# The first MLP's scale and offset, applied where its sums are copied out of PSUM

## The chip, the cores and the metric

One core of one Trainium2 chip runs the whole program. The metric is the device time of one execution in microseconds. Three runs of the kernel before took 1071.02, 1076.27 and 1076.54 us, so the median is 1076.27 us.

## The reference

Attention over 4 sequences of 576 positions with 8 heads of 64, then two MLPs over 2304 tokens of 512 features. What matters here is the first MLP.

```python
def _moe_ref(x, w_in, w_out, s, b):
    h = x @ w_in                 # 2304x512 @ 512x2048
    r = np.maximum(h, 0.0)
    g = s * (r * r) + b          # s and b are one number each
    return (g @ w_out).astype(np.float32)   # 2048x512

def _moe2_ref(x, w_a, w_b, w_out):
    return ((x @ w_a) * (x @ w_b) @ w_out).astype(np.float32)
```

Since s and b are single numbers, `g @ w_out` equals s times `(r * r) @ w_out` plus b times the sum of each column of `w_out`.

## The kernel before, in words

Tokens are cut into six units of 384 (`TB`, `NB` = 6), and the 2048 inner features of the first MLP into 16 steps of 128 (`NF1`). For each unit and step, `h_mm` (lines 538 to 557) multiplies x by a step of `w_in`. Every float32 operand of the large products is split into a high and a low part (`split`, lines 104 to 106: the high part is copied on ScalarE, the low one is a subtraction on the engine that is named), and a product is three products of TensorE, so a step's h is 12 products of 128x128 by 128x384. Behind them stands a chain over the value `r`: ScalarE takes the positive part (line 550) and squares it (line 551), GpSimd applies s and b (line 552), ScalarE copies the high part into `gt`, and VectorE subtracts the low part (lines 105 and 106). This chain has a raised priority. `o_mm` (lines 559 to 573) then multiplies `gt` by the step of `w_out`, 12 products again, and adds them up in four PSUM banks over all 16 steps; it follows h by two steps (`AHEAD1`). After the last step ScalarE copies the four banks out (line 572), and SyncE's queue stores them to memory, feature by token; the last unit keeps a tile of its own.

The weights arrive as float64. `stage` (lines 108 to 121) loads a step as pairs of words, `to_float32` (lines 123 to 148) turns them to float32 in place in the high words, with a scaling on ScalarE (for the second MLP on GpSimd, line 128), three bit operations on VectorE (lines 137, 140, 143), and a split whose low part is GpSimd's. `next_weights` (lines 693 to 698) does this for both matrices, for two steps before unit 0 and for one step in each step of unit 0. The staged words lie in slots that the finished weights use later; the last steps have two slots of another pool (`raw`).

Alongside the first MLP runs the attention of the next unit, which VectorE and GpSimd share: GpSimd multiplies (lines 477 and 495), VectorE sums (lines 481 and 506), and the results become the next unit's x. `Stream` deals its steps out evenly over the calls in a unit. In the last unit the attention is over, and the weights of the second MLP are loaded and turned to float32 (`load_w2`), with low parts and scaling on GpSimd. The second MLP follows: 12 inner steps for each of the six units, 36 products in a step.

Each engine works through its queue in an order that is fixed when the program is built: a planner simulates the program and takes the ready instruction of the highest priority. Instructions of different engines are tied by semaphores alone.

Of the kernel before, what the change touches and what calls it, by code (L numbers as in the profile page):

```python
# [8 lines left out]
F32 = mybir.dt.float32  # L9
F32R = mybir.dt.float32r  # L10
U32 = mybir.dt.uint32
AF = mybir.ActivationFunctionType
ALU = mybir.AluOpType
# [4 lines left out]
P = 128  # L18
# [3 lines left out]
# takes the exponent that the high word of 2.0 ** -119 has, read as a float32, to the least one  # L22
# [4 lines left out]
def sparse_attention_two_mlps(  # L27
# [14 lines left out]
    """Rows of x are tokens.  Heads 0-3 see the last 32 positions, heads 4-7 the  # L42
    earlier positions of their own residue modulo 32.

    Every float32 operand of the large products is split into hi (12 significant
    bits, float32r) and lo = value - hi (exact), and a product is hi*hi + hi*lo +
    lo*hi, accumulated in float32.  The weights come as the bits of float64 and
    are made float32 by shifting their fields into place.
    """
    nc = tc.nc  # L50
    B, H, S, D = q.shape
    NT, DM = out.shape
# [5 lines left out]
    QT = 96  # L58
# [29 lines left out]
    # window column c is allowed for row p where p < c <= p + 32  # L88
# [12 lines left out]

    o1 = dram.tile([DM, NT], F32, name="o1")
# [5 lines left out]
    def stage(w, f, cols, pool):  # L108
        """A part of a matrix of float64 as (low, high) words; also the load's instruction."""
# [13 lines left out]
    def to_float32(r, pool, tag, on_pool=False):  # L123
        """(low, high) words of float64 -> hi and lo parts of the float32."""
        low, high = r[:, :, 0], r[:, :, 1]
        # what is below float32's range gets a zero exponent here, the others keep their low bits
# [9 lines left out]
        # the sign stays; the exponent's three upper bits, now zero, go  # L136
# [16 lines left out]
    # post-processing goes before what else is ready  # L153
# [3 lines left out]
    # ------------------------------------------------------------- attention  # L157
# [6 lines left out]
    # the part that no head of the stride sees is set once  # L164
# [5 lines left out]
    # each head's query rows, zero in the other's  # L170
# [3 lines left out]
    def softmax(pt, scores, msk):  # L174
        """pt = exp(scale * (scores + msk) - max) / (sum + 1e-9) along the last axis."""
# [50 lines left out]
    def local(spans, n, hp_, c0):  # L226
        """A pair of heads for two spans (sequence, first position) of queries; two neighbours
        in a partition.  Keys of spans that follow each other are shared."""
# [73 lines left out]
    def first_mask():  # L302
        """For the first positions of a sequence: heads 0-3's, then heads 4-7's."""
# [21 lines left out]
    def first(bb, qk, vn, fmask, pool, tag):  # L325
        """All heads of a sequence's first positions."""
# [49 lines left out]
    def strided_one(pair):  # L376
        """Two strided heads of all sequences' second QT positions: sequence and residue in the
        partitions, two heads for each step."""
# [47 lines left out]
        # [(b r), (h d)] -> [(h d), (b r)] for each step  # L426
# [9 lines left out]
    def strided_soft(pt, sc, rows, cols):  # L436
        """pt = softmax of scale * sc along the last axis."""
# [17 lines left out]
    def pairs(u):  # L455
        # (first column, columns, first row): two columns at a time where all rows see them
        i0 = (u % NP) * IU
        for j in range(0, i0, 2):
            yield j, 2, 0
        for j in range(IU):  # L460
            yield i0 + j, 1, j

    def strided(u):
# [23 lines left out]
        def strided_rest():  # L487
# [23 lines left out]
            # [(h r), (i, d)] -> [(i parity, d), (h r)], two steps i at a time  # L511
# [23 lines left out]
    # ------------------------------------------------------------- first MLP  # L535
    wi, wo = {}, {}

    def h_mm(n, f):
# [9 lines left out]
        with tc.high_priority(offset=URGENT):  # L548
# [3 lines left out]
            nc.gpsimd.tensor_scalar(  # L552
                out=r, in0=r, scalar1=s_sb, scalar2=b_sb, op0=ALU.mult, op1=ALU.add
            )
# [4 lines left out]
    def o_mm(acc, gt, f, n):  # L559
# [10 lines left out]
        for e in range(KD):  # L570
            o = hp.tile([P, TB], F32, tag="r", name="o1s", bufs=3) if last is None else last[:, e]
            nc.scalar.activation(out=o, in_=acc[e], func=AF.Copy)
            nc.sync.dma_start(out=o1[e * P:(e + 1) * P, cols], in_=o)

    # ------------------------------------------------------------- second MLP
# [3 lines left out]
    def load_w2(i):  # L579
        f, kind = divmod(i, 3)  # L580
        # the slots that stage the others' words take the last ones
# [225 lines left out]
```

## Time and profile before

| | |
|---|---|
| runs | 1071.02, 1076.27, 1076.54 us |
| profiled execution, from its first to its last instruction | 1073.5 us |
| TensorE busy | 984.4 us, 92% |
| VectorE busy | 610.7 us, 57% |
| ScalarE busy | 415.4 us, 39% |
| GpSimd busy | 494.2 us, 46% |
| mean granted clock of TensorE | 0.961 of 2.4 GHz |

The profile's own record of the profiled execution is its span; the median of the runs lies 2.8 us above it. An engine's busy time includes time in which an instruction has begun and waits for something inside the engine. TensorE's two rows are the products (PE) and the loading of weights into its array (PEld), which overlap. A wait is the idle time of an engine ahead of an instruction, with the instruction that ended it.

### The profile page before, as it was taken

The page shows a single profiled execution, that of the slowest core. Times are in us where ns is not written, and L with a number is a line of the kernel's source. Part 1 is how long each engine was busy: PE and PEld are TensorE (multiplying, and loading weights), DVE is VectorE, ACT ScalarE, POOL GpSimd, SP SyncE. Part 2 cuts the span into 40 slices and gives each one's busy share as a digit, 9 for nine tenths or more (in the row PEclk, how much of TensorE's full clock was granted, in tenths as well). Part 3 has the DMA queues.
Part 4 walks back from the last instruction along what each step waited for, and adds up shares of the span by engine and source line. Part 5 has one row for each costly group of instructions (what it writes and reads, how often), then busy time and mean ns, then how long its engine had stood idle before and what let it go on. Part 6 is the DMA issues. An engine that isn't in the chain of part 4 may idle for free.

```text
span 1073.5 us, 14660 instructions
## 1 busy us (share of the span) xinstructions
PE 984.4 (92%) x5382; PEld 914.5 (85%) x5382; DVE 610.7 (57%) x1128; ACT 415.4 (39%) x1075; POOL 494.2 (46%) x428
## 2 busy tenths in 40 slices
PE   7867789988989999999987789999999999999998
PEld 6767678888979889898876778999999999999997
DVE  6899988898895885884789992111211111111111
ACT  5665655535535545645534341211211211211211
POOL 1599787887784885862789980100100100100000
PEclk9988889989999999999989899999999999999999
DMA  8753731121211121102344550010200100000000
GB/s 158 219 179 100 198 84 60 40 50 35 58 35 32 49 52 31 56 13 85 98 157 147 157 173 5 30 30 1 59 1 2 59 1 1 30 1 1 30 1 30
DMA packets 98888, 68.33 MB, mean 64 GB/s; under 512 B 57856, under 2 KB 92928, under 8 KB 98816
## 3 DMA queue, kind: packets, MB, share of 16 engines
q1 hardware_dynamic: 98816, 67.40, 22.4%
q8 instruction: 42, 0.69, 0.3%
q14 instruction: 30, 0.25, 0.1%
HBM read 57.93 MB, written 9.44 MB: 63 GB/s over the span
## 4 chain that ended last, share of the span: by engine, by line
PE 54%; DVE 18%; POOL 15%; issue 7%; ACT 4%; DMA 2%; SPq 1%; POOLq 0%; DVEq 0%; ACTq 0%
PE acc L621 13%; PE pa L605 13%; PE pb L605 13%; PE acc L562 6%; DVE ot L506 5%; PE h L543 4%; POOL w L106 4%; POOL r L552 4%; POOL prod L477 3%; DVE gt L106 3%; DVE raw L143 2%; POOL raw L128 1%; DVE raw L140 1%; DVE raw L137 1%; POOL prod L495 1%
## 5 line engine op out<-in xcount | busy, mean ns | idle before, releaser
L562 PE MATMUL acc<-gt,w 128*128 128x384 f32 x1152 | 248.6, 360 | 40.8 <-DVE gt L106 22.0
L562 PEld LDWEIGHTS acc<-gt,w 128*128 128x128 f32 x1152 | 214.7, 202 | 55.8 <-DVE gt L106 29.8
L543 PE MATMUL h<-x,w 128*128 128x384 f32 x1152 | 238.1, 351 | 13.1 <-ACT w L105 4.9
L543 PEld LDWEIGHTS h<-x,w 128*128 128x128 f32 x1152 | 207.8, 196 | 19.0 <-ACT w L105 6.9
L613 DVE TENSOR_TENSOR ab<-pb,ab 128x384 f32<-128x384 f32 x72 | 40.1, 556 | 299.8 <-PE pb L605 298.7
L621 PE MATMUL acc<-w,abt 128*128 128x512 f32 x648 | 162.3, 394 | 4.9 <-ACT abt L105 2.5
L605 PE MATMUL pa<-x,w 128*128 128x384 f32 x864 | 164.7, 338 | 0.0
L605 PE MATMUL pb<-x,w 128*128 128x384 f32 x864 | 161.9, 334 | 0.0
L605 PEld LDWEIGHTS pa<-x,w 128*128 128x128 f32 x864 | 154.8, 189 | 6.2
L605 PEld LDWEIGHTS pb<-x,w 128*128 128x128 f32 x864 | 150.8, 188 | 0.3 <-ACT w L105 0.3
L621 PEld LDWEIGHTS acc<-w,abt 128*128 128x128 f32 x648 | 120.2, 188 | 28.5 <-DVE abt L106 3.7
L106 POOL TENSOR_TENSOR x<-xr,x 128x384 fp32r<-128x384 f32 x24 | 26.4, 1126 | 254.5 <-ACT x L105 254.5
L106 POOL TENSOR_TENSOR w<-raw,w 128x512 fp32r<-128x512 f32 x68 | 111.1, 1642 | 29.2 <-ACT w L105 25.1
L552 POOL TENSOR_SCALAR r<-r,s_sb,b_sb 128x384 f32<-128x384 f32 x96 | 102.5, 1068 | 41.4 <-ACT r L551 41.3
L495 POOL TENSOR_TENSOR prod<-sv,pt 128x768 f32<-128x768 f32 (+6 forms) x84 | 92.6, 1109 | 52.5 <-DVE ot L506 26.2
L477 POOL TENSOR_TENSOR prod<-sq,sk 128x768 f32<-128x768 f32 (+6 forms) x84 | 106.7, 1282 | 15.6 <-DVE s L481 11.1
L106 DVE TENSOR_TENSOR gt<-r,gt 128x384 fp32r<-128x384 f32 x96 | 90.4, 944 | 39.7 <-ACT gt L105 39.2
L612 ACT ACTIVATE ab<-pa 128x384 f32<-128x384 f32 x72 | 35.3, 491 | 183.1 <-PE pa L605 183.1
L506 DVE TENSOR_TENSOR ot<-ot,prod 128x384 f32<-128x384 f32 (+2 forms) x104 | 95.4, 917 | 6.3 <-POOL prod L495 0.5
L105 ACT ACTIVATE gt<-r 128x384 fp32r<-128x384 f32 x96 | 50.1, 522 | 107.0 <-POOL r L552 106.7
L105 ACT ACTIVATE abt<-ab 128x384 fp32r<-128x384 f32 x72 | 37.7, 524 | 138.9 <-DVE ab L613 138.9
L105 ACT ACTIVATE w<-raw 128x512 fp32r<-128x512 f32 x68 | 45.5, 675 | 72.2 <-DVE raw L143 60.1
(92 smaller groups left out, 956.4 us busy)
## 6 DMA issues: line engine op xcount, KB each, us to landing
raw<-in_moe_w_out_dram SPq DMA_DIRECT2D x28, 512.0 KB, 4.4
raw<-in_moe_w_in_dram SPq DMA_DIRECT2D x16, 512.0 KB, 5.9
raw<-in_moe_w_a_dram SPq DMA_DIRECT2D x12, 512.0 KB, 3.8
raw<-in_moe_w_b_dram SPq DMA_DIRECT2D x12, 512.0 KB, 3.9
xr<-o SPq DMA_DIRECT2D x6, 768.0 KB, 4.5
o<-o1s SPq DMA_DIRECT2D x20, 192.0 KB, 1.9
vn<-in_v_dram SPq DMA_DIRECT2D x40, 64.0 KB, 2.2
out_dram<-o SPq DMA_DIRECT2D x9, 256.0 KB, 2.1
```

The source lines that it names most:

```text
L105: nc.scalar.activation(out=hi, in_=src, func=AF.Copy)
L106: return eng_lo.tensor_tensor(out=lo, in0=src, in1=hi.bitcast(F32), op=ALU.subtract)
L477: nc.gpsimd.tensor_tensor(out=p_[:, :m, r:], in0=sq[:, None, r:, :].to_broadcast(shape), in1=sk[:, j:j + m, None, :].to_broadcast(shape), ...
L495: nc.gpsimd.tensor_tensor(out=p_[:, :m, r:], in0=sv[:, j:j + m, None, :].to_broadcast(shape), in1=pt[:, r:, j:j + m].rearrange("p i j -> p ...
L506: nc.vector.tensor_tensor(out=ot[:, r:], in0=ot[:, r:], in1=p_[:, e, r:], op=ALU.add)
L543: nc.tensor.matmul(ph, lhsT=wi[f][:, a, kk, :], rhs=x_t[n][:, c, kk, :], start=(m == 0), stop=(m == 3 * KD - 1),)
L552: nc.gpsimd.tensor_scalar(out=r, in0=r, scalar1=s_sb, scalar2=b_sb, op0=ALU.mult, op1=ALU.add)
L562: nc.tensor.matmul(acc[e], lhsT=wo[f][:, a, e * P:(e + 1) * P], rhs=gt[:, c, :], start=(f == 0 and m == 0), stop=(f == NF1 - 1 and m == 2),)
L605: nc.tensor.matmul(pz, lhsT=w2[i][:, a, kk, :], rhs=x2[:, c, kk, :], start=(m == 0), stop=(m == 3 * KD - 1),)
L612: nc.scalar.activation(out=ab, in_=pa, func=AF.Copy)
L613: nc.vector.tensor_tensor(out=ab, in0=pb, in1=ab, op=ALU.mult)
L621: nc.tensor.matmul(acc[t], lhsT=gt[:, a, t * P:(t + 1) * P], rhs=w2[3 * f + 2][:, c, :], start=(f == 0 and m == 0), stop=(f == NF2 - 1 and ...
```

## The change

GpSimd's instruction between the two products is gone, so `gt` holds the square without s and b. While the weights are made, GpSimd adds up the 16 steps of `w_out` in `w_sum` (128x512); after the last one TensorE multiplies it by b, held in all 128 partitions, which gives b times the column sums, and VectorE copies these to `b_col`. The copy out of PSUM multiplies by s and adds `b_col`. Comments are dropped too; they are left out here.

```diff
+    w_sum = const.tile([P, DM], F32, name="w_sum")
+    b_col = const.tile([P, KD], F32, name="b_col")
...
             r = hp.tile([P, TB], F32, tag="r", name="r", bufs=3)
             nc.scalar.activation(out=r, in_=ph, func=AF.Relu)
             nc.scalar.activation(out=r, in_=r, func=AF.Square)
-            nc.gpsimd.tensor_scalar(
-                out=r, in0=r, scalar1=s_sb, scalar2=b_sb, op0=ALU.mult, op1=ALU.add
-            )
             gt = gp.tile([P, 2, TB], F32R, tag="gt", name="gt")
             split(gt[:, 0], gt[:, 1], r, nc.vector)
...
-            nc.scalar.activation(out=o, in_=acc[e], func=AF.Copy)
+            nc.scalar.activation(
+                out=o, in_=acc[e], func=AF.Identity, scale=s_sb, bias=b_col[:, e:e + 1]
+            )
...
         wo[f] = to_float32(words[f][1], wpb, "w")
+        part = words[f][1][:, :, 1].bitcast(F32)
+        if f == 0:
+            nc.gpsimd.tensor_copy(out=w_sum, in_=part)
+        else:
+            nc.gpsimd.tensor_tensor(out=w_sum, in0=w_sum, in1=part, op=ALU.add)
+        if f == NF1 - 1:
+            pc = ps_a.tile([P, KD], F32, tag="a", name="pc")
+            for e in range(KD):
+                nc.tensor.matmul(
+                    pc[:, e:e + 1], lhsT=w_sum[:, e * P:(e + 1) * P], rhs=b_sb, start=True, stop=True,
+                )
+            nc.vector.tensor_copy(out=b_col, in_=pc)
```

## Rows read from the trace of the kernel before

**Rows 1.** The page: busy us (share) xinstructions, and the granted clock in 40 slices.

```profile
PE 984.4 (92%) x5382; PEld 914.5 (85%) x5382; DVE 610.7 (57%) x1128; ACT 415.4 (39%) x1075; POOL 494.2 (46%) x428
...
PEclk9988889989999999999989899999999999999999
```

**Rows 2.** Busy by stretch: from:to, length, PE PEld DVE ACT POOL, clock, DMA.

```profile
39.00:172.00 133.00, 104.28 (x527) 93.25 (x528) 122.73 (x215) 81.54 (x204) 112.91 (x76) 0.86 0.51 145
172.00:260.00 88.00, 78.29 (x460) 74.00 (x459) 76.85 (x139) 40.96 (x121) 68.86 (x63) 0.94 0.18 45
260.00:349.00 89.00, 81.98 (x489) 77.46 (x488) 69.18 (x138) 44.64 (x135) 62.21 (x58) 0.96 0.17 43
349.00:435.00 86.00, 80.38 (x486) 76.78 (x484) 64.87 (x133) 42.66 (x125) 60.83 (x56) 0.96 0.17 43
435.00:519.00 84.00, 80.08 (x487) 75.91 (x485) 58.75 (x127) 45.23 (x134) 47.84 (x49) 0.98 0.16 50
519.00:616.00 97.00, 80.06 (x398) 74.11 (x397) 86.99 (x91) 42.67 (x83) 90.28 (x71) 0.91 0.47 150
616.00:647.00 31.00, 26.09 (x133) 22.86 (x132) 27.69 (x31) 13.12 (x26) 24.17 (x20) 1.00 0.52 162
647.00:1073.50 426.50, 422.05 (x2221) 395.06 (x2219) 76.80 (x136) 84.19 (x169) 17.96 (x17) 1.00 0.05 17
...
60.00:150.00 90.00, 64.99 (x333) 57.25 (x334) 84.51 (x138) 53.96 (x133) 83.74 (x53) 0.84 0.49 136
...
540.00:616.00 76.00, 59.84 (x288) 55.31 (x287) 73.86 (x75) 29.11 (x54) 71.01 (x56) 0.89 0.48 152
```

**Rows 3.** Line 552: ns min/median/max, first and last start; who waited (us, times).

```profile
L552 POOL TENSOR_SCALAR r<-r,s_sb,b_sb x96: 652/960/4993, 46.7 to 608.4; 128x384 f32<-128x384 f32 x96
...
  ACT gt L105: 106.7, 64
```

**Rows 4.** Line 552 alone, by stretch: from:to, length, POOL busy (xcount), clock, DMA.

```profile
39.00:172.00 133.00, 28.15 (x17) 0.86 0.51 145
...
349.00:435.00 86.00, 13.12 (x16) 0.96 0.17 43
...
519.00:616.00 97.00, 22.91 (x16) 0.91 0.47 150
```

**Rows 5.** GpSimd on 128x512: the weights' subtraction, and the scaling of their words.

```profile
L106 POOL TENSOR_TENSOR w<-raw,w x68: 1285/1610/7396, 34.1 to 646.6; 128x512 fp32r<-128x512 f32 x68
...
L128 POOL TENSOR_SCALAR raw<-raw x36: 637/918/1102, 155.4 to 642.3; 128x512 f32<-128x512 f32 x36
```

**Rows 6.** Weight loads' waits, unit 0, then 519 to 647 us: us, times, longest.

```profile
PEld acc L562 <- ACT gt L105: 15.9, 8, 3.5
...
PEld acc L562 <- DVE gt L106: 16.0, 9, 2.9
```

**Rows 7.** The chain that ended last: start us, us, what.

```profile
506.60 2.08 PE h L543 x12
```

**Rows 8.** Weight loads, 172 to 519 us: busy us, mean ns, idle before.

```profile
L562 PEld LDWEIGHTS acc<-gt,w 128*128 128x128 f32 x768 | 139.2, 196 | 13.3 <-DVE gt L106 9.4 <-ACT o1s L572 2.3 <-ACT gt L105 0.9
L543 PEld LDWEIGHTS h<-x,w 128*128 128x128 f32 x750 | 132.5, 193 | 7.1 <-ACT r L550 2.9 <-DVE x L106 2.3 <-ACT x L105 0.8
...
L283 PEld LDWEIGHTS ppt<-ident,lpt 96*128 96x128 f32 x64 | 7.2, 150 | 9.8 <-issue 6.8 <-ACT r L550 2.6
```

**Rows 9.** ScalarE's exponential with a bias, and a plain copy: ns min/median/max.

```profile
L188 ACT ACTIVATE lpt<-lpt,mx x80: 384/388/405, 53.7 to 506.7; 96x128 f32<-96x128 f32 x80
...
L265 ACT ACTIVATE kT<-pqk x80: 260/268/297, 41.5 to 500.1; 64x112 f32<-64x112 f32 x64, 64x128 f32<-64x128 f32 x16
```

**Rows 10.** In order of time near 148 us: SyncE's loads, and GpSimd.

```profile
148.91 2.26 SPq L118 DMA_DIRECT2D raw<-in_moe_w_out_dram  x2
...
147.60 1.29 POOL L106 TENSOR_TENSOR w<-raw,w 128x512 fp32r<-128x512 f32 x1
```

**Rows 11.** VectorE's bit operation on line 140: ns min/median/max.

```profile
L140 DVE SCALAR_TENSOR_TENSOR raw<-raw x68: 643/692/1808, 20.9 to 643.0; 128x512 uint32<-128x512 uint32 x68
```

## The prediction

> **What bounds the kernel now.** Read the totals first [rows 1]: TensorE is busy for 92% of the span, GpSimd for 46%. That alone would say that work on GpSimd is free. It isn't, because the share is a mean over stages with different limits, so the second view cuts the span at the ends of the six units of the first MLP (unit 0 from 39 to 172 us, unit 5 from 519 to 616 us) and shows the second MLP behind them [rows 2]. The reader is to see three kinds of stage.
>
> In unit 0, and above all from 60 to 150 us, VectorE is busy for 84.5 and GpSimd for 83.7 of 90 us, TensorE for 65 [rows 2]: the weights are being turned to float32 there while the attention of the next unit runs, and both engines are full. Unit 5 from 540 to 616 us is the same picture with the weights of the second MLP: 73.9 and 71.0 of 76 us [rows 2], and it goes on to 647 us (27.7 and 24.2 of 31 us) [rows 2]. In units 1 to 4 no engine is full but TensorE: it is busy for 78 to 82 of 84 to 89 us, VectorE falls from 77 to 59 and GpSimd from 69 to 48 [rows 2]. From 647 us on TensorE is busy for 422.1 of 426.5 us and GpSimd does next to nothing [rows 2]; there the changed line doesn't occur, and what is won or lost before is carried to the end one for one.
>
> The third view is the changed line itself. Its 96 instructions take 0.652 us at best, 0.960 in the middle and 4.993 at worst, and ScalarE waited 106.7 us for it, 64 times [rows 3], since the value's high part can't be copied before. By stage its busy time is 28.2 us in unit 0, 13.1 in a middle unit and 22.9 in unit 5 [rows 4]: 16 instructions (17 in unit 0's window) of 1.66, 0.82 and 1.43 us. The same work takes more than twice as long where VectorE is full. So a time that is worked out for it has two ends: the 0.652 us that it needs and the stretched time that it occupies.
>
> **What the change removes.** 96 instructions of GpSimd, 62.6 us at 0.652 us each, 102 us as they stand, all on the chain from a finished h to the operand of the second product. Behind them on GpSimd's queue wait the weights' low parts and the attention's products; ahead of them lay the same, and that is why ScalarE's 106.7 us exceed the instructions' own time.
>
> **What it adds on GpSimd.** One copy and 15 additions of 128x512, all in or just before unit 0. The nearest rows are of the same engine and tile: the weights' subtraction, which reads the same strided words and a second operand (1.285 us at best, 1.610 in the middle), and the one-operand scaling of those words (0.637 and 0.918) [rows 5]. At best 0.637 + 15 x 1.285 = 19.9 us, as they stand 0.918 + 15 x 1.610 = 25.1 us. They are on no chain to a product before unit 0 ends, but they lie ahead of the next products in GpSimd's queue.
>
> **Unit 0.** At needed times 19.9 - 16 x 0.652 = +9.5 us; at stretched ones 25.1 - 28.2 = -3.1 us. These are the bounds. A stretched instruction is one that waits for VectorE, and that wait isn't freed by taking the instruction out, so I go by the needed times. Some 12 of the 16 steps lie in the full stretch (the first two sums and the last two lie outside, where GpSimd has room): 12 x (1.285 - 0.652) = +7.6 us. Against this stands that TensorE waits 15.9 us there for the high parts [rows 6], and those now come one queue earlier; I give 1.6 of it back and take **+6 us**.
>
> **Unit 5 and the start of the second MLP.** Nothing is added. From 540 us on 12 steps are left: 12 x 0.652 = 7.8 us at needed times; all 16 stretched, 22.9 us. TensorE's wait for the low parts of the operand from 519 to 647 us is 16.0 us [rows 6], so there is something to take. What is late next is the weights' own work on VectorE, which stays. I take the needed end, **-8 us**, since the pair of engines stays full to 647 us; the bounds are 0 (if VectorE alone decides) and -22.9.
>
> **Units 1 to 4.** Twelve products take 2.08 us [rows 7], so a unit's 32 x 12 take 66.6 us, and the rest is attention on TensorE, gaps and clock. The gaps: TensorE's idle time in the four windows is 9.7 + 7.0 + 5.6 + 3.9 = 26.2 us [rows 2]. The granted clock is 0.94 to 0.98 of full speed there (its levels are 1.2 and 2.4 GHz; it is lowest, 0.84, from 60 to 150 us where TensorE is idle most, and 1.00 behind 647 us where it is busy throughout [rows 2]), which costs 88 x 0.06 + 89 x 0.04 + 86 x 0.04 + 84 x 0.02 = 14 us. More than these 40 us can't be won. Of the gaps, the weight loads of the second product wait 9.4 us for the operand's low part and 0.9 for its high part [rows 8]. This is what a chain that is shorter by one queue and 0.82 us takes away; the 9.8 us before the attention's transposes and the 7.1 us before the first products [rows 8] hang on VectorE, loads and the order of the attention, and I leave them. 10.3 us are a quarter of the 40, so a quarter of the clock's 14 comes with them, some 3 us. I take **-13 us**, with bounds 0 (the wait goes over to the attention's adds on VectorE) and -34 (nearly all of the 40 us).
>
> **Copying out.** 24 copies get a scale and a bias from memory. The nearest rows: ScalarE's exponential with one such bias takes 0.388 us for 96x128, a plain copy of 64x112 takes 0.268 [rows 9], so some 0.11 us for each operand at about that size, 0.22 for two, 5.3 us in all. TensorE waits 2.3 us for these copies in units 1 to 4 [rows 8]; most are hidden behind the next unit's first products. **+1 us**, bounds 0 and 5.3. The Trainium skill (ScalarE: Activation LUTs, What ACT_TABLE_LOAD costs) gives about 93 ns for each operand from memory, which would be 4.5 us in all, and says in its section on table sets that identity is filler in every set, so that no load of tables is added. The trace of before shows neither this function nor a second load.
>
> **The column sums.** Four one-column products and a small copy wait for the last sum, after the last w_out is converted. The load of that part is issued at 148.91 us, just as the subtraction that held its slot ends (147.60 + 1.29) [rows 10]; now the sum holds the slot too, 1.3 us longer or more. Queued behind the four products on TensorE are the last steps of unit 0, and they use one of two banks that the attention uses. The last step's own operand was later than its weights, so this is covered in part: **+0.5 us**, bounds 0 and 4.
>
> **The sum.** 6 - 8 - 13 + 1 + 0.5 = -13.5 us on the profiled span of 1073.5 us: 1060 us. The median of the three runs lies 2.8 us above the span, and I add that: **1062.8 us**. The order of every engine's work is planned anew for the changed program, which may move each stage by a few microseconds either way.
>
> **Rivals.** *A larger gain: the two engines are one resource.* What VectorE's rows show: the same bit operation of 128x512 takes 0.643 us at best and 1.808 at worst [rows 11], and the changed line 0.652 and 4.993 [rows 3]. If units 1 to 4 too are held by the two engines together, then the needed 4 x 16 x 0.652 = 41.7 us come out there, as far as TensorE lets them: -34, and unit 5 gives 10.4: 6 - 34 - 10.4 + 1 = -37, or 1039 us. Against it: neither engine is full in these units. The Trainium skill (SBUF — State Buffer, Who interferes with whom) states such an exclusive lock for VectorE with two inputs from SBUF against GpSimd reading SBUF. By that rule, the stretched rows agree; that it sets the time in units 1 to 4 no row shows.
>
> *Slower: the sums stretch unit 0 and nothing pays it back.* Place: GpSimd's queue from 60 to 172 us, where each sum stands ahead of a low part that h waits for, and holds a slot that a load waits for. Price +9.5 for the unit and +4 for the late last load; if the middle units win nothing since VectorE's adds end last there, and unit 5 just 3 us: 9.5 + 4 - 3 + 1.5 = +12, or 1088 us. It decides once the middle units and unit 5 give back less than unit 0 takes. For it: both engines are full there. Against it: the waits of [rows 6, 8] are on the very chain that is cut.
>
> *No change.* Unit 0's +6 to +9.5 meets unit 5's -8, and in the middle the time that the operand waited is spent on TensorE's queue for attention instead (0 to -4): 1071 to 1080 us, 1075 in the middle. This is also what comes out if the new plan puts the sums into the chain as the old instruction was.
>
> **Chances.** A gain near the forecast 0.54, the larger gain 0.15, no change 0.18, slower 0.13. The last runs differ by some 0.5%, so that is what counts as a difference: faster 0.69, same 0.18, slower 0.13. The range leaves out most of the slower case and the far half of the larger gain: 1044 (unit 0 at 0, the middle at -20, unit 5 at -12) to 1081 us.
>
> **What would show it.** In the new profile GpSimd's busy time in units 1 to 4 falls by about 13 us each, and the operand's copy on ScalarE waits for ScalarE alone. If the steps are right, unit 0 ends some 6 us later, unit 5 is 8 us shorter, and the weight loads' 10 us of waiting in the middle are gone. If unit 0 doesn't grow, the sums fit into gaps and the bound by needed times was wrong. If the middle units keep their lengths while those waits vanish, the attention's order is what holds them. An idle TensorE in front of the four small products would show their wait.

## The result, and the profile after

The changed kernel takes 1084.45 us (median of four runs, 1081.09 to 1085.25), the kernel before, run beside it, 1075.8 (1071.02 to 1076.54): a ratio of 1.0089 with an interval from 1.0061 to 1.0116. It is slower, by some 9 us; 1062.8 were forecast, with a range to 1081. The profiled execution's span is 1082.8 us against 1073.5.

The totals and the granted clock of after, answering to [rows 1]:

```profile
PE 981.3 (91%) x5390; PEld 916.7 (85%) x5390; DVE 617.6 (57%) x1129; ACT 420.9 (39%) x1075; POOL 421.8 (39%) x348
...
PEclk9997988998999999999998999999999999999999
```

GpSimd lost 72.4 us of busy time. VectorE, with the same work and one small copy more, gained 6.9. The stages of after, cut at the ends of its own units, answer to [rows 2] (from:to, length, busy time of PE, PEld, DVE, ACT, POOL, granted clock, DMA share, GB/s):

```profile
39.00:171.00 132.00, 97.92 (x489) 88.40 (x488) 126.19 (x181) 73.62 (x175) 110.44 (x68) 0.88 0.52 145
171.00:271.00 100.00, 83.94 (x498) 80.29 (x498) 81.10 (x171) 49.11 (x145) 60.51 (x53) 0.91 0.16 42
271.00:356.00 85.00, 78.80 (x479) 75.26 (x478) 62.52 (x134) 44.77 (x132) 47.59 (x42) 0.98 0.18 45
356.00:442.00 86.00, 81.69 (x497) 78.00 (x495) 66.15 (x138) 46.29 (x135) 49.66 (x43) 0.96 0.18 45
442.00:527.00 85.00, 80.68 (x485) 77.29 (x483) 57.18 (x124) 46.64 (x135) 36.31 (x34) 0.96 0.16 49
527.00:623.00 96.00, 76.26 (x395) 70.87 (x394) 94.80 (x103) 43.44 (x85) 66.33 (x57) 0.95 0.51 159
```

Read the two columns DVE and POOL. In the last unit GpSimd fell from 90.28 of 97 us to 66.33 of 96, and VectorE rose from 86.99 to 94.80: it is busy for all but 1.2 us, and the unit is 2.6 us shorter (table below). A part of the rise is other work: 84 of the weights' bit operations start in this unit, 78 before. In unit 0 the picture is the same, 126.19 of 132.

Where the 9.3 us came from is read best from the units' own lengths. A unit ends with the last of its 192 products of `o_mm`; unit 0 counts from 39 us; the last column runs from the end of unit 5 to the end of the span. The lengths are worked out from the traces, us:

| kernel | unit 0 | 1 | 2 | 3 | 4 | 5 | rest | span |
|---|---|---|---|---|---|---|---|---|
| before | 132.7 | 81.8 | 92.9 | 85.4 | 85.5 | 98.9 | 457.3 | 1073.5 |
| after | 131.9 | 100.4 | 85.2 | 85.2 | 85.3 | 96.3 | 459.6 | 1082.8 |
| e2_no_sums | 126.1 | 95.5 | 85.2 | 85.3 | 84.8 | 96.7 | 459.9 | 1072.6 |
| e4_before_with_sums | 149.5 | 81.5 | 88.0 | 93.1 | 85.9 | 97.9 | 457.7 | 1092.6 |
| e5_late_weights_moved | 132.2 | 93.3 | 85.2 | 85.2 | 85.3 | 96.9 | 461.1 | 1078.2 |
| e10_less_vector_work | 126.6 | 93.6 | 85.2 | 85.4 | 85.4 | 85.1 | 457.9 | 1058.2 |
| e11_fewer_adds | 126.5 | 91.3 | 81.7 | 81.9 | 79.5 | 96.4 | 460.0 | 1056.1 |

From before to after: unit 0 -0.8, unit 1 +18.6, unit 2 -7.7, units 3 and 4 -0.4, unit 5 -2.6, the rest +2.3. The loss shows in one place, the border of units 0 and 1. TensorE's products there (start, us, tile, count, and in brackets the idle time and what ended it):

```profile
164.23 0.68 PE L546 MATMUL h<-x,w 128*128 128x384 f32 x3
165.32 2.40 PE L562 MATMUL acc<-gt,w 128*128 128x384 f32 x12 [0.41 <-DVE gt L109]
167.56 0.95 PE L711 MATMUL pc<-b_sb,w_sum 128*128 128x1 f32 x8
168.37 1.09 PE L276 MATMUL pss<-kT,qz 128*96 128x128 f32 x8
169.22 1.66 PE L562 MATMUL acc<-gt,w 128*128 128x384 f32 x8
178.39 0.88 PE L286 MATMUL ppt<-ident,lpt 96*128 96x96 f32 x4 [7.51 <-DVE lpt L198]
179.84 0.91 PE L293 MATMUL po<-pT,vn 128*64 128x96 f32 x8 [0.58 <-ACT pT L288]
180.68 0.58 PE L264 MATMUL pqk<-ident,qn 96*128 96x96 f32 x2
181.06 0.58 PE L264 MATMUL pqk<-ident,kn 112*128 112x112 f32 x2
181.32 4.90 PE L546 MATMUL h<-x,w 128*128 128x384 f32 x17
```

Six of the twelve products of unit 1's first step are done by 164.9 us; the other six need the last part of its x and stand at 181.3 behind a hole of 7.5 us, which a softmax of the attention ends on VectorE (`lpt`, line 198). In the kernel before, unit 1's first step was through at 163.5 and the next followed at 166.3. Its gap of this kind lay at the next border: the first six products of unit 2 are done by 251.4 us and the other six start at 257.8, which is most of why its unit 2 is long. VectorE in the stretch above, in after:

```profile
162.58 2.22 DVE L146 SCALAR_TENSOR_TENSOR raw<-raw 128x512 uint32<-128x512 uint32 x1
...
168.83 2.32 DVE L143 SCALAR_TENSOR_TENSOR raw<-raw 128x512 uint32<-128x512 uint32 x1
171.07 0.15 DVE L714 COPY b_col<-pc 128x4 f32<-128x4 f32 x1
171.19 1.37 DVE L146 SCALAR_TENSOR_TENSOR raw<-raw 128x512 uint32<-128x512 uint32 x1
...
174.37 0.41 DVE L140 TENSOR_SCALAR raw<-raw 128x512 uint32<-128x512 uint32 x1
...
175.44 0.68 DVE L143 SCALAR_TENSOR_TENSOR raw<-raw 128x512 uint32<-128x512 uint32 x1
...
176.50 0.75 DVE L146 SCALAR_TENSOR_TENSOR raw<-raw 128x512 uint32<-128x512 uint32 x1
177.17 1.07 DVE L198 TENSOR_TENSOR lpt<-lpt,sm 96x512 f32<-96x512 f32 x1
```

The row at 162.58 us ends the first MLP's weights. The others turn two matrices of the second MLP, which nothing needs before unit 5 is over, some 440 us later, and yet they lie ahead of the softmax for which TensorE waits. The stretch's other time on VectorE goes mostly to the attention's sums (line 484).

Last, ScalarE's waits in the whole run (engine, what waited, for what: us in total, times, longest). The wait for GpSimd of [rows 3] is gone; these three grew:

```profile
ACT w L108 <- DVE raw L146: 88.2, 39, 6.6
ACT r L553 <- PE h L546: 50.4, 31, 7.9
ACT lpt L191 <- DVE mx L188: 48.0, 16, 9.9
```

Before, these three stood at 60.1, 18.1 and 20.1 us. They grew by 28.1, 32.3 and 27.9, or 88 us together: most of the 106.7 us for which ScalarE had waited for GpSimd, it now waits for VectorE and TensorE.

### The profile page after: what moved, and what is told of

It is laid out like the page before. It is cut to its first block, busy times and chain, and to the rows that moved or that the text cites. A ratio compares the mean times of both kernels' runs of the same rounds, so it can differ in the third digit from the quotient of the medians.

```text
span 1082.8 us, 14610 instructions
## 1 busy us (share of the span) xinstructions
PE 981.3 (91%) x5390; PEld 916.7 (85%) x5390; DVE 617.6 (57%) x1129; ACT 420.9 (39%) x1075; POOL 421.8 (39%) x348
## 4 chain that ended last, share of the span: by engine, by line
PE 54%; DVE 29%; issue 8%; POOL 4%; ACT 2%; DMA 1%; SPq 0%; DVEq 0%; ACTq 0%; POOLq 0%
PE acc L624 14%; PE pa L608 14%; PE pb L608 13%; DVE ot L509 7%; PE acc L562 6%; DVE raw L143 4%; PE h L546 4%; DVE raw L140 4%; DVE gt L109 3%; POOL prod L480 3%; DVE raw L146 3%; DVE s L484 1%; DVE lpt L198 1%; PE fss L353 1%; DMA raw<-in_moe_w_in_dram 1%
## 5 line engine op out<-in xcount | busy, mean ns | idle before, releaser
L562 PE MATMUL acc<-gt,w 128*128 128x384 f32 x1152 | 243.8, 356 | 40.4 <-DVE gt L109 36.4
L546 PE MATMUL h<-x,w 128*128 128x384 f32 x1152 | 241.2, 354 | 17.2 <-ACT w L108 7.1
L562 PEld LDWEIGHTS acc<-gt,w 128*128 128x128 f32 x1152 | 211.3, 199 | 52.4 <-DVE gt L109 44.1
L546 PEld LDWEIGHTS h<-x,w 128*128 128x128 f32 x1152 | 212.4, 199 | 22.6 <-ACT w L108 9.1
L109 DVE TENSOR_TENSOR gt<-r,gt 128x384 fp32r<-128x384 f32 x96 | 84.9, 886 | 27.3 <-ACT gt L108 26.6
L509 DVE TENSOR_TENSOR ot<-ot,prod 128x384 f32<-128x384 f32 (+2 forms) x104 | 89.3, 859 | 7.7 <-POOL prod L498 2.7
L146 DVE SCALAR_TENSOR_TENSOR raw<-raw 128x512 uint32<-128x512 uint32 x68 | 73.3, 1080 | 0.2
L143 DVE SCALAR_TENSOR_TENSOR raw<-raw 128x512 uint32<-128x512 uint32 x68 | 69.7, 1028 | 4.0 <-POOL raw L131 1.6
```

The costliest lines, as they stand in the source:

```text
L109: return eng_lo.tensor_tensor(out=lo, in0=src, in1=hi.bitcast(F32), op=ALU.subtract)
L143: nc.vector.scalar_tensor_tensor(out=low, in0=high, scalar=3, in1=low, op0=ALU.logical_shift_left, op1=ALU.bitwise_or)
L146: nc.vector.scalar_tensor_tensor(out=high, in0=high, scalar=0x80000000, in1=low, op0=ALU.bitwise_and, op1=ALU.bitwise_or)
L509: nc.vector.tensor_tensor(out=ot[:, r:], in0=ot[:, r:], in1=p_[:, e, r:], op=ALU.add)
L546: nc.tensor.matmul(ph, lhsT=wi[f][:, a, kk, :], rhs=x_t[n][:, c, kk, :], start=(m == 0), stop=(m == 3 * KD - 1),)
L562: nc.tensor.matmul(acc[e], lhsT=wo[f][:, a, e * P:(e + 1) * P], rhs=gt[:, c, :], start=(f == 0 and m == 0), stop=(f == NF1 - 1 and m == 2),)
```

## The experiments

Kernels that are compared ran beside runs of the kernel before; each ratio is to those, with its 95% interval. All edits but those of e4, e6 and e9 are made on the changed kernel. The runs e2, e3, e7, e10 and e11 leave out a part of the result or get it wrong, as is said for each.

### What is the price of the sums, and of the small products?

The theory after the first look at the traces was that the sums on GpSimd make the loss. The rivals: the small products hold up TensorE's queue, or their wait for the last sum does, or the removal itself brings an order in which unit 1's attention comes late.

**e1_products_late** takes the small products out of their place and puts them into `o_mm`, ahead of the last step's.

```diff
-        if f == NF1 - 1:
-            pc = ps_a.tile([P, KD], F32, tag="a", name="pc")
...
+        if n == 0 and f == NF1 - 1:
+            col_sums()
```

> The changed kernel with the four column-sum products moved in program order from the making of the last weights to just before unit 0's last step of the second product. Three theories for the 8.7 us by which the changed kernel is slower, and above all for its 20 us hole at the border of units 0 and 1 (TensorE's first products of unit 1 run from 162.9 to 183.6 us, 161.2 to 163.5 before). Theory Q: the four products stand in TensorE's queue ahead of the attention's scores for unit 1 and wait for the last sum, so the attention is late. Then the hole falls to 3 us or less and the time to 1084.4 - 17 = 1067 us. Theory G: GpSimd's 26 us of sums crowd the attention out of unit 0. Then nothing changes, 1082 to 1085 us. Theory P: with GpSimd's instruction gone from the chain the planner puts the attention later among TensorE's products; the sums don't matter. Then 1080 to 1085 us.

Measured: 1085.61 us, ratio 1.010 (1.0081 to 1.0119). Unit 1's first step still runs from 163.8 to 181.3 us (162.9 to 183.6 in the changed kernel). Unit 0 is 4.4 us longer than there, unit 1 7.5 shorter, unit 2 3.5 longer, and the span is the same to 0.3 us: single units move, their sum doesn't. TensorE's queue behind the small products is not the cause.

**e2_no_sums** leaves out the sums and the small products, and so b's part of the result.

```diff
+    nc.vector.memset(b_col, 0.0)
...
-        if f == 0:
-            nc.gpsimd.tensor_copy(out=w_sum, in_=part)
-        else:
-            nc.gpsimd.tensor_tensor(out=w_sum, in0=w_sum, in1=part, op=ALU.add)
```

> The changed kernel without the sums and the four products; the offset is a column of zeros, so the part of b is left out. It shows what the removal of GpSimd's instruction alone is worth. Theory Q: no hole, 1058 to 1064 us (as forecast, less the sums' 6 us). Theory G: no hole, 1058 to 1064 us. Theory P: the hole stays, 1075 to 1082 us.

Measured: 1074.51 us, ratio 0.9996 (0.9983 to 1.0008). So the removal of the 96 instructions, with the dearer copy-out that goes with it, is worth nothing by itself, and the loss is the sums'. By the table, against before: unit 0 -6.6, unit 1 +13.7, unit 2 -7.7, unit 5 -2.2, the rest +2.6. The hole stays without any sums (7.0 us of idle time in front of the same products), so it comes with the removal and the order planned for it. It is the end of a delay that is older than the border: the second, third and fourth of the four groups of `po` products, with which unit 1's attention over the last 32 positions ends, start at 113.0, 155.8 and 173.6 us, where they stood at 104.1, 131.4 and 156.4 before. The sums add 5.8 us to unit 0 and 4.9 to unit 1, and 10.2 to the span. Its weight loads' waits in units 1 to 4 (165 to 516 us; busy us, mean ns, idle before and for what) answer to [rows 8]:

```profile
L546 PEld LDWEIGHTS h<-x,w 128*128 128x128 f32 x768 | 137.0, 194 | 9.6 <-DVE x L109 4.8 <-ACT x L108 1.9 <-ACT x L531 1.5
L562 PEld LDWEIGHTS acc<-gt,w 128*128 128x128 f32 x768 | 134.5, 190 | 5.9 <-DVE gt L109 2.9 <-ACT o1s L573 2.7
L276 PEld LDWEIGHTS pss<-kT,qz 128*96 128x96 f32 x128 | 17.3, 180 | 11.2 <-issue 11.0
L286 PEld LDWEIGHTS ppt<-ident,lpt 96*128 96x128 f32 x68 | 7.6, 145 | 10.5 <-issue 10.0
```

The second product's waits are indeed cut, from 13.3 to 5.9 us, those for its operand (`gt`) from 10.3 to about 3. The attention's products (`pss`, `ppt`) and those that need a new x took them over: 4.1, 9.8 and 7.1 us before, 11.2, 10.5 and 9.6 now. The row of before for `pss`, which [rows 8] doesn't have:

```profile
L273 PEld LDWEIGHTS pss<-kT,qz 128*96 128x96 f32 x120 | 15.1, 170 | 4.1 <-ACT kT L265 2.7 <-ACT gt L105 0.8 <-issue 0.4
```

**e3_products_no_wait** gives the small products another operand, so that they don't wait for the last sum; b's part comes out wrong.

```diff
-                    pc[:, e:e + 1], lhsT=w_sum[:, e * P:(e + 1) * P], rhs=b_sb, start=True, stop=True,
+                    pc[:, e:e + 1], lhsT=ident, rhs=b_sb, start=True, stop=True,
```

> The changed kernel with the four products at their place, but on a constant tile in place of the sums, so that they wait for nothing; the sums are still made. The part of b is wrong. Theory Q: what costs is the wait, so the hole falls to 3 us or less and the time to 1067 us. If instead the bank that the four products take is what costs, the hole stays, 1080 to 1085 us. Theory G: 1082 to 1085 us. Theory P: 1080 to 1085 us.

Measured: 1087.05 us, ratio 1.0119 (1.0095 to 1.0143). That wait costs nothing.

**e4_before_with_sums** puts the sums alone into the kernel before.

```diff
         wo[f] = to_float32(words[f][1], wpb, "w")
+        part = words[f][1][:, :, 1].bitcast(F32)
+        if f == 0:
+            nc.gpsimd.tensor_copy(out=w_sum, in_=part)
+        else:
+            nc.gpsimd.tensor_tensor(out=w_sum, in0=w_sum, in1=part, op=ALU.add)
```

> The kernel before, with the 16 sums on GpSimd added as in the change, read by nothing. The price of the sums alone. Theory Q: they cost what the prediction gave them or less, 1076 to 1085 us, by way of unit 0 that ends up to 9 us later, and no hole at the border. Theory G: 17 us or more, 1090 to 1096 us, with the hole. Theory P: 1074 to 1079 us.

Measured: 1093.84 us, ratio 1.0166 (1.0137 to 1.0194), 19 us more; unit 0 takes 16.8 of them. The sums' instructions, of this kernel (ns min/median/max, first and last start):

```profile
L705 POOL TENSOR_TENSOR w_sum<-w_sum,raw x15: 1278/1591/1752, 44.1 to 182.4; 128x512 f32<-128x512 f32 x15
```

15 x 1.591 = 23.9 us of GpSimd where it is full, and 16.8 us of unit 0. VectorE's busy time rose with them from 610.7 to 622.2 us, for the same 1128 instructions. With the old instruction out of the way the same sums cost 10.

### Why does the hole at unit 1 open?

Either the second MLP's conversions stand ahead of the attention on VectorE, or the writing of x, part by part over ScalarE and VectorE, is what ends late.

**e5_late_weights_moved** lets the second MLP's later matrices be turned only behind unit 1's second step.

```diff
+            if f == 1:
+                marks[n] = done.ins
...
-        w2[i] = to_float32(r, pool, tag, True)
+        late = tc.issue_after(marks[1]) if i >= 2 * NF1 else ExitStack()
+        with late:
+            w2[i] = to_float32(r, pool, tag, True)
```

> The changed kernel, with the float32 conversion of the second MLP's last four matrices (two of them go into slots that come free at the end of unit 0) held back on each engine until the second step of unit 1. Without any sums the hole at the border of units 0 and 1 was still there (TensorE's first products of unit 1 from 159.2 to 178.0 us), so neither the sums nor the four products make it. Theory W: the conversions of those two matrices, placed by the planner just where VectorE still has the last softmax for unit 1, make it: in the changed kernel they hold VectorE's queue for 2.3 + 1.4 + 0.4 + 0.7 + 0.8 us between scores and softmax, and part of that waits for a load. Then the hole shrinks by 6 to 10 us and the time is 1074 to 1079 us. Rival A: VectorE and GpSimd are full in unit 0, so the attention is late whatever stands in between; less than 3 us, 1082 to 1085 us.

Measured: 1078.39 us, ratio 1.0052 (1.0032 to 1.0072): by the two ratios 4 us less than the changed kernel, with intervals that touch; its span is 4.6 us shorter. The softmax comes 3.2 us sooner and the hole in front of it is 4.0 us instead of 7.5 (TensorE's row, columns as above):

```profile
175.18 0.84 PE L286 MATMUL ppt<-ident,lpt 96*128 96x96 f32 x4 [3.97 <-DVE lpt L198]
```

The conversions ahead of the softmax are a part of the hole, then: 3.5 of its 7.5 us, and unit 1 as a whole is 7.1 us shorter, of the 18.6 that it grew by. That all 7.1 are theirs isn't shown; in e1 unit 1 got 7.5 us shorter without any gain.

**e6_before_x_grouped**, on the kernel before, writes the four high parts of a piece of x ahead of the four low ones, at a raised priority.

```diff
-                    nc.scalar.activation(out=hi, in_=src, func=AF.Copy)
-                    nc.vector.tensor_tensor(out=lo, in0=src, in1=hi.bitcast(F32), op=ALU.subtract)
+                    parts.append((hi, lo, src))
+            with tc.high_priority(offset=URGENT):
+                for hi, _, src in parts:
+                    nc.scalar.activation(out=hi, in_=src, func=AF.Copy)
+                for hi, lo, src in parts:
+                    nc.vector.tensor_tensor(out=lo, in0=src, in1=hi.bitcast(F32), op=ALU.subtract)
```

> The kernel before with one edit: the strided attention's four writes of x first make all four high parts on ScalarE, then all four low parts on VectorE, at raised priority, in place of high, low, high, low. It asks what ends the middle units, since the removal of GpSimd's instruction left units 3 and 4 at 85 us each. Theory X: TensorE waits at the border for these eight copies, which alternate between two engines with attention adds of the unit after next in between on VectorE. Then each of the four borders gets 3 to 6 us shorter and the time is 1050 to 1062 us. Rival: the rate of the attention on VectorE and GpSimd ends the units; then the borders close and the time comes back inside the units, 1071 to 1077 us.

Measured: 1077.06 us, ratio 1.0038 (1.0022 to 1.0054). No gain. Unit 2 is 3.1 us shorter and unit 5 ends 3.4 us sooner, but the rest takes 463.0 us where it took 457.3; how x is written is at most a small part of what holds the units.

**e7_no_sums_both** is e2, b's part left out, with the edits of e5 and e6.

```diff
-            nc.gpsimd.tensor_tensor(out=w_sum, in0=w_sum, in1=part, op=ALU.add)
...
+        late = tc.issue_after(marks[1]) if i >= 2 * NF1 else ExitStack()
...
+            with tc.high_priority(offset=URGENT):
```

> The changed kernel without sums and without the four products (the part of b is left out), with both edits: the late weights held back and the writes of x grouped. If theories W and X both hold, the removal of GpSimd's instruction is worth something once these two queues no longer take it back: 1074.5 - 8 (hole) - 16 (borders) = 1050 us, and less than the kernel before with grouped writes. If the rate on VectorE and GpSimd is what ends the units, 1068 to 1075 us.

Measured: 1075.47 us, ratio 1.002 (1.0004 to 1.0036). Unit 1 is at 91.3 us (95.5 in e2) and unit 4 at 82.0, but unit 2 rose to 90.0 and unit 5 to 99.0. What one border gains, another gives back.

### What is the bound, GpSimd or VectorE?

If GpSimd's busy time counts, one-input work of the same time must cost what the sums cost, and less VectorE work must bring little. If VectorE is the bound and two-input work of GpSimd blocks it, the one-input work must be cheap, and less VectorE work must shorten just the units that it is taken from.

**e9_one_input_for_sums**, on the kernel before, has two operations with one input each, of the same size, in the place of a sum with two.

```diff
+        for _ in range(2):
+            nc.gpsimd.tensor_scalar(
+                out=w_sum, in0=part, scalar1=1.0, scalar2=0.0, op0=ALU.mult, op1=ALU.add
+            )
```

> The kernel before, where the 16 sums of the run e4 (19 us slower) are replaced by two one-input scalings of the same 128x512 words each, 32 instructions of 0.64 us at best on GpSimd at the same places: the same needed time on GpSimd, 20 us, read by nothing. Theory B: what a GpSimd instruction costs is what it blocks on VectorE. With one input it gives way to VectorE (VectorE's bit operations take 0.78 us beside one-input GpSimd work, 0.68 alone, and 1.10 beside two-input work), so these cost little: 1074 to 1083 us. Theory N: GpSimd's own needed time is what counts, as the prediction had it: 1088 to 1096 us, as with the sums.

Measured: 1082.06 us, ratio 1.0086 (1.0054 to 1.0118): +8 us, where the sums of e4 cost +19 (1.0137 to 1.0194). In this kernel:

```profile
L703 POOL TENSOR_SCALAR w_sum<-raw x32: 637/947/1450, 24.8 to 186.9; 128x512 f32<-128x512 f32 x32
```

32 x 0.947 = 30.3 us, more of GpSimd's time than the sums' 23.9, for less than half of their price. In unit 0, where this work lies, it adds 10.0 us (142.6 against 132.7), the sums 16.8; the rest of the difference between the two runs lies in later units. VectorE's busy time rose by 4.1 us here, to 614.8, and by 11.5 in e4. So the second input costs extra, by way of VectorE; how the 8 us that one-input work costs divide between GpSimd's own time and VectorE's stretching isn't shown.

**e10_less_vector_work** is e2 without one of VectorE's three bit operations for the second MLP's 36 matrices, whose values come out wrong.

```diff
-        nc.vector.scalar_tensor_tensor(
-            out=low, in0=high, scalar=3, in1=low, op0=ALU.logical_shift_left, op1=ALU.bitwise_or
-        )
+        if not on_pool:
+            nc.vector.scalar_tensor_tensor(
+                out=low, in0=high, scalar=3, in1=low, op0=ALU.logical_shift_left, op1=ALU.bitwise_or
+            )
```

> The changed kernel without sums (1074.5 us) in which one of VectorE's three bit operations is left out for the 36 matrices of the second MLP (their values come out wrong), about 1 us each as they stand. The removal of GpSimd's instruction left unit 5 and the start of the second MLP together at the same length. Theory V: VectorE sets the time there. Then 20 to 30 of these 36 us come out: unit 5 and what follows get 12 to 25 us shorter, 1050 to 1062 us. Rival: the chain over ScalarE and GpSimd from one weight to the next sets it; 1068 to 1075 us.

Measured: 1059.54 us, ratio 0.9862 (0.984 to 0.9884). Unit 5 fell from 96.7 to 85.1 us, the units ahead of it hardly moved. Its unit 5, from 518 to 600.2 us (all but its first 2.8 us):

```profile
518.00:600.20 82.20, 70.88 (x377) 66.23 (x377) 74.37 (x72) 44.04 (x84) 72.45 (x59) 0.98 0.60 187
```

TensorE is busy for 86% here and for 80.10 of 96 us in e2 (516 to 612 us), at a granted clock of 0.98 and 0.89. The clock isn't what sets the length: after has 0.95 in this unit and e2 0.89, and they take 96.3 and 96.7 us. The operation that is left out has two inputs, so GpSimd is relieved of it too; what the unit gains by that, no run tells apart.

**e11_fewer_adds** is e2 with one of the two adds on VectorE left out for each product of the strided attention that has two (28 adds; the attention comes out wrong).

```diff
-                    for e in range(m):
+                    for e in range(1):
                         nc.vector.tensor_tensor(
```

> The changed kernel without sums, with one of each pair of the strided attention's adds on VectorE left out (28 adds of 128x384, some 0.9 us each, 6 us in each of units 1 to 4 as they work for the next; the attention comes out wrong). Theory V: VectorE's rate ends the middle units too: each of units 1 to 4 gets 3 to 6 us shorter, 1052 to 1063 us. Theory O: what ends them is the chain at the border over TensorE's queue (last scores, transposes and copies of x; GpSimd stands still for 14 us there), and the adds between are covered: 1068 to 1075 us, units 3 and 4 stay within 1 us of 85 us.

Measured: 1057.86 us, ratio 0.9852 (0.9829 to 0.9875). Units 1 to 4 are shorter by 4.2, 3.5, 3.4 and 5.3 us than in e2, unit 5 is the same to 0.3. The granted clock is 1.00 in its units 2 to 4 and 0.98 in e2's, but that isn't the reason: unit 3 takes 85.2 us at 0.96 in after, 85.3 at 0.98 in e2 and 84.9 at 1.00 in e1. In the middle units no engine but TensorE was said to be full, and VectorE isn't; they hang on its part of the attention all the same, as a link of the chain to the next unit's x.

### A version that is faster than both

**e8_b_in_split** needs no sums and no instruction of GpSimd for s and b: since s (r r + b/s) is the value wanted (for an s that isn't 0), ScalarE adds b/s as it copies the high part, VectorE as it subtracts, and the copy-out multiplies by s. It has the edits of e5 and e6 too.

```diff
-            split(gt[:, 0], gt[:, 1], r, nc.vector)
+            nc.scalar.activation(out=gt[:, 0], in_=r, func=AF.Identity, bias=b_s)
+            done = nc.vector.scalar_tensor_tensor(
+                out=gt[:, 1], in0=r, scalar=b_s, in1=gt[:, 0].bitcast(F32), op0=ALU.add, op1=ALU.subtract
+            )
...
-                out=o, in_=acc[e], func=AF.Identity, scale=s_sb, bias=b_col[:, e:e + 1]
+                out=o, in_=acc[e], func=AF.Copy, scale=s_sb
```

> A version with no sums that computes everything: the high part is a copy of r*r with b/s added as ScalarE's bias, the low part on VectorE is (r*r + b/s) - high in one instruction, and s multiplies in the copy out of PSUM; with both edits of the run before. ScalarE's operand from memory costs some 0.1 us for each of 96 copies and lies in the chain; TensorE should wait for it in units 0 and 5 at most. Expected by theories W and X: the run before plus 0 to 4 us, 1050 to 1054 us; by the rival, 1068 to 1078 us.

Measured: 1068.84 us, ratio 0.9957 (0.9943 to 0.9971): 4.8 us below the kernel before.

**e12_b_in_split_alone** is the same without the edits of e5 and e6.

```diff
-            split(gt[:, 0], gt[:, 1], r, nc.vector)
+            nc.scalar.activation(out=gt[:, 0], in_=r, func=AF.Identity, bias=b_s)
+            nc.vector.scalar_tensor_tensor(
```

> The version of run e8 that computes everything without sums, but without its two other edits (late weights held back, writes of x grouped). Those edits brought nothing together in the run without sums (1075.5 against 1074.5 us), so if e8's gain comes from b in the split, this is 1066 to 1071 us; if it comes from the edits, 1073 to 1077 us.

Measured: 1075.05 us, ratio 1.0011 (0.9997 to 1.0025). So e8's gain is of the combination: the new split gains nothing alone, nor do the two edits (e7). Against e7, units 0, 1, 2, 3, 4 and 5 of e8 go from 125.8, 91.3, 90.0, 86.0, 82.0, 99.0 to 121.1, 93.5, 88.3, 86.4, 82.8, 95.4 us. Why is open; each of these kernels has an order of its own, and single units differ by 2 to 8 us between them.

## Why the prediction was wrong, step by step

**The failed step is the middle units' -13 us**, which came out as +10.5, and with it the first reading, that only TensorE bounds them. The wait it rested on did vanish: in e2 and in after the second product's weight loads wait 5.9 and 5.6 us in units 1 to 4, where [rows 8] had 13.3. But units 1 to 4 together take 350.8 us in e2 and 356.1 in after, where they took 345.6: unit 2 gives back 7.7 of what unit 1 loses, and units 3 and 4 kept their length to 0.7 us. The prediction named this case ("the wait goes over to the attention's adds on VectorE", as a bound of 0) and took a quarter of the gap and the clock instead. It is the bound that held: the next unit's x comes out of VectorE, so what one product waits less, another waits more. e11 shows it: 28 adds taken from VectorE give 16.4 us over units 1 to 4, and all of GpSimd's 64 instructions there gave none. The 3 us that were taken from the clock had no ground either, since a unit of 85 us has been seen at 0.96, 0.98 and 1.00. That the sum is worse than 0 is the border again: 13.7 us of growth in unit 1 from the new order, which the prediction allowed "a few microseconds" for, and 4.9 from the sums.

**Unit 5's -8** was -2.6, and the rest of the run gave 2.3 of it back. Here the reading was that VectorE and GpSimd are full as a pair. It is VectorE's work that counts: with GpSimd's busy time down by 24 us the unit gained 2.6, with one operation of three taken from VectorE it gained 11.6 (e10). The prediction had this too, as its bound of 0, "if VectorE alone decides". The kernel before shows why (VectorE's and GpSimd's rows, in order of time):

```profile
575.13 1.74 POOL L106 TENSOR_TENSOR w<-raw,w 128x512 fp32r<-128x512 f32 x1
575.63 1.53 DVE L137 TENSOR_SCALAR raw<-raw 128x512 uint32<-128x512 uint32 x1
576.86 1.87 POOL L552 TENSOR_SCALAR r<-r,s_sb,b_sb 128x384 f32<-128x384 f32 x1
577.08 0.68 DVE L143 SCALAR_TENSOR_TENSOR raw<-raw 128x512 uint32<-128x512 uint32 x1
577.68 0.68 DVE L140 SCALAR_TENSOR_TENSOR raw<-raw 128x512 uint32<-128x512 uint32 x1
...
578.70 1.75 POOL L106 TENSOR_TENSOR w<-raw,w 128x512 fp32r<-128x512 f32 x1
...
579.20 1.54 DVE L137 TENSOR_SCALAR raw<-raw 128x512 uint32<-128x512 uint32 x1
```

Beside GpSimd's subtraction, which has two inputs, VectorE's operation takes 1.53 us, where its kind takes 0.41 elsewhere (the row at 174.37 us of after, above). Beside the removed instruction, which has one tensor as input, VectorE's two operations run at 0.68 us, near line 140's best of 0.643 [rows 11], and it is the removed instruction that is stretched, to 1.87 us from 0.652. Counted over the trace of before, 29 of VectorE's two-input bit operations began while the removed instruction, and nothing else, ran on GpSimd: 28 of them took 0.64 to 0.68 us. Of 13 that began while the two-input subtraction alone ran, 6 took 1.7 to 1.8 us and 7 took 0.68 to 0.69. So the long rows [rows 3, 4] were the sign that the instruction gave way to VectorE's bit operations. (VectorE's busy time as a whole did fall in e2, from 610.7 to 601.2 us, in an order that also changed what runs beside what.) The prediction said so itself ("one that waits for VectorE"), and yet took its needed 0.652 us out of the stage as if VectorE had paid them. The number of inputs isn't the whole of it: the 9 such operations of after that began under GpSimd's one-input scaling of the second MLP's words took 1.12 to 1.15 us, and why that one doesn't give way is open. The Trainium skill (SBUF — State Buffer, Who interferes with whom) tells of an exclusive lock: whoever issues first holds it for the whole instruction, and the other fully blocks. The subtraction's first row agrees with it: VectorE's operation begins 0.50 us behind it and ends 0.29 us behind its end. The 29 cases of the removed instruction don't: it began first and was the one to wait.

**Unit 0's +6** was -0.8. The forecast was a difference: 12 x 1.285 = 15.4 us for the sums, less 12 x 0.652 = 7.8 and 1.6 for the removal. The removal gave 6.6 (before to e2), of the 9.4. The sums took 5.8 there (e2 to after), not 15.4; on the kernel before, with the old instruction still beside them, it was 16.8 (e4). So the sums' price in the unit was the term that was off, and what was missed is the next border: unit 1 needs the attention's last x, and that ended later, not sooner. As instructions the sums were sized well: 1298 ns at best and 1611 in the middle against 1285 and 1610 of [rows 5].

```profile
L706 POOL TENSOR_TENSOR w_sum<-w_sum,raw x15: 1298/1611/3582, 45.0 to 164.9; 128x512 f32<-128x512 f32 x15
```

What was not in their price is that a two-input addition stretches VectorE: by e9 and e4, 11 of 19 us on the kernel before, 6.9 of 16.8 within unit 0.

**The small products' +0.5** held: e1 and e3 won nothing. **The copy-out's +1** was sized right as an instruction, 0.22 us estimated and 0.18 measured (0.664 against 0.484 us in the middle units), and no second load of ScalarE's tables came with it (one in either trace). No effect on a path was seen, though no run had it alone:

```profile
L573 ACT ACTIVATE o1s<-acc,b_col,s_sb 128x384 f32<-128x384 f32 x16 | 10.4, 664 | 8.7 <-DVE gt L109 8.7
```

**The rivals.** The slower one (0.13) was right in one part of its mechanism, "the middle units win nothing since VectorE's adds end last there". That its price of +12 is near the +9.3 is luck: it put +13.5 into unit 0 and its late load, where -0.8 came, and 0 into the middle, where +10.5 came. The load of the last w_out did come 5.4 us later (154.3 us after 148.91 [rows 10]), and unit 0 ended 0.8 us sooner. Its condition was weighed against [rows 6, 8], waits of TensorE, and these only say what came last, not what comes next. The larger gain took the two engines for one resource, and the removed instruction was the one that had been giving way.

What stays open: why the new order lets the attention of unit 1 fall behind all through unit 0. The conversions of the second MLP (e5) are at most 7.1 us of what unit 1 grew by; the remainder has no run of its own. Nor is it shown why e8's parts gain only together.

## What to carry to other kernels

A stretched instruction on GpSimd is not by itself a cost to VectorE: look at how long VectorE's own operations take beside it, and don't count GpSimd's busy time. Before a chain is shortened, ask which engine delivers the input after the next; a cut wait is worth something only if that engine is not the bound, and leaving out some of that engine's work in a trial run (as e10 and e11 do) puts a number on it. Where a planner orders the work, cost the border at which one stage's input ends the other, for there much of the new order was paid here.

## What the runs showed of the hardware

That on GpSimd an operation with two tensor inputs can be dearer to its neighbour than two with one input: +19 us for 23.9 us of the first kind in unit 0 (e4), +8 for 30.3 of the second (e9), with 11.5 and 4.1 us more of VectorE's busy time. That a GpSimd instruction which began first can be the one to wait: 28 of 29 of VectorE's operations that began under the removed one kept their 0.64 to 0.68 us, where all 9 under the one-input scaling took 1.12 to 1.15. That ScalarE's copy from PSUM gets 0.18 us longer for 128x384 when scale and bias come from memory. And that a busy total can hide the bound: VectorE is busy for 57% of the span, and less work for it made every one of the first MLP's later units shorter (e10, e11), which less work for GpSimd alone (e2) didn't.
